# Attention and feed-forward on one core: the remainder of the exponential as the square of a logarithm, the sums over keys from one matrix product, the feed-forward's linear part as one matrix

## The chip, the cores and the metric

The program runs on one core of one Trainium2 chip, in one launch. The metric is the device time of one execution in microseconds. Three runs of the kernel before took 1280.52, 1281.53 and 1281.73 us; the median is 1281.53 us.

## The reference, cut to what matters

Keys and values are one tensor: `kv` is averaged over 4 x 4 places, which leaves 768 keys in each of the 4 batches, and multiplied by `w_sr`. Each batch has 12288 queries of 128 channels. A feed-forward layer with 2048 hidden units follows.

```
kv_pool = kv.reshape(B, H//4, 4, W//4, 4, C).mean(axis=(2, 4))
k = v = kv_pool.reshape(B, -1, C) @ w_sr              # 768 x 128 in each batch
s = (q @ k.T) / sqrt(C);  a = softmax(s)
x = a @ v                                             # 49152 tokens x 128
h = x @ w_in                                          # 2048 hidden units
return (h - tanh(h)) @ w_out
```

## The kernel before, in words

**The arithmetic.** Scores are small here, and so is the distance of a token's `x` from the mean of the values. The kernel subtracts the mean of the keys, and writes exp(s) as 1 + s + r. The part 1 contributes nothing to the centred values, the part s contributes a product of the query with one 128 x 128 matrix of the batch (`Mh`, the second moment of the values), and only the remainder r = exp(s) - 1 - s needs the work per key. In the same way h - tanh(h) is taken about the mean value: a constant and a slope (`At`, `Ah`, one matrix for the batch) and a rest, which is u * u * (u + 1) of a scaled u and needs the work per hidden unit. At the end a flag says whether the two approximations hold for these inputs (`NEAR`, `SPREAD`); if it is 0, a general path (`any_inputs`) computes everything again.

**The tiling.** A tile is 512 queries, channels on partitions; there are 24 tiles in a batch and 96 in all. A "wide" array has 128 x 1024 elements: 3 of them cover the 768 keys, 8 the 2048 hidden units. `big` is a ring of 3 wide PSUM buffers (2 banks each), `x` and `acc` are one bank each: that is all of PSUM.

**Attention of one tile** (`attention`). ScalarE rounds the query to fp32r (L879, `qr`), GpSimd forms what rounding left (L932, `ql`). For each of 3 wide arrays TensorE makes scores (L894, 2 matmuls), ScalarE the exponential (L898), VectorE the remainder r in fp16 (L901). The sum of the remainders over keys is needed for the softmax's denominator: from tile 2 on, the first array is copied by a DMA on SP's queue into `rs` and the other two are added to it by accumulating DMAs that GpSimd issues (L917); TensorE then sums `rs` over partitions with a matrix of ones (L922, 2 matmuls). ScalarE makes the factor 1/denominator from it (L942), the numerator is 6 matmuls with the fp16 values (L938) and 3 for the linear part in two precisions (L928), VectorE multiplies (L949), GpSimd rounds the result (L952) and forms the rest (L978).

**Feed-forward of one tile** (`feed_forward`). 16 matmuls make the hidden units, two to a `big` buffer (L1009). For 7 of the 8 wide arrays ScalarE squares (L1013) and VectorE multiplies (L1016). For the eighth (`ON_POOL`) ScalarE copies (L1020) and GpSimd does three operations (L1023, L1027 twice). 16 matmuls bring the result back (L1047), 3 add the linear part in two precisions (L998), ScalarE adds the constant (L1058), SP stores.

**Once per batch** (`keys`, `about_centre`): the pooled keys (DMAs that add on arrival, issued by GpSimd, L463), key and value matrices, moments, slopes and scaled weights. For batches 1 to 3 this work stands between the tiles of the batch before; for batch 0 it stands at the start.

**What sets the order.** All operations are first listed with a step (a place in time, 8 steps to a tile, table `AT`), an engine and a cost. `Plan.run` then plays them through once at build time and writes each engine's instructions in the order in which they started there. On the chip that order is fixed: an engine that waits holds up everything behind it on its queue. `lane` operations of an engine start in the order of their steps. `MOVES` shifts single operations of the start and of the batch work. Steps rank the work and are no times.

## Time and profile before

| | |
|---|---|
| span of the profiled execution | 1278.4 us |
| median of the three runs | 1281.53 us |
| TensorE busy | 1246.3 us (97%), 5424 matmuls |
| VectorE busy | 1220.1 us (95%), 1180 instructions |
| ScalarE busy | 1200.0 us (94%), 1426 |
| GpSimd busy | 1160.8 us (91%), 981 |
| granted TensorE clock, mean of the span | 0.995 |

The profile gives one time for the profiled execution, its span from the first to the last instruction; the median of the timed runs is 3.1 us above it. A busy share is the union of the instructions' spans. A matmul's listed duration (about 0.39 us) overlaps that of the next, so its cost is read as the distance from one start to the next; the same holds for short overlaps on the other engines. Of two spans on GpSimd that overlap, only the starts are exact.

### The profile page before, as it was taken

How to read it: one execution, taken by the hardware profiler on the slowest of the kernel's cores; microseconds unless marked ns; L12 is line 12 of the kernel's file. 1: busy time of each engine (PE TensorE's matmuls, PEld its weight loads, DVE VectorE, ACT ScalarE, POOL GpSimd, SP SyncE). 2: the span in 40 equal slices, each digit the busy share in tenths (PEclk: the TensorE clock that was granted, in tenths of full speed). 3: DMA queues.
4: the chain of work that ended last, by engine and by line, in shares of the span. 5: the costliest groups of instructions: out<-in, count | busy, mean ns of one | idle time of the engine just before them, and what ended most of it. 6: DMA issues, size and time to landing. Idle time of an engine off the chain costs nothing.

```text
span 1278.4 us, 17185 instructions
## 1 busy us (share of the span) xinstructions
PE 1246.3 (97%) x5424; PEld 869.0 (68%) x5424; DVE 1220.1 (95%) x1180; ACT 1200.0 (94%) x1426; POOL 1160.8 (91%) x981
## 2 busy tenths in 40 slices
PE   4999999999999999999999999999999999999997
PEld 3766766676667676676676666677767667676765
DVE  6899999999999999999999999999999999999996
ACT  4799999999999999999999999999999999999995
POOL 3689999999999998999999998999998888988886
PEclk9999999999999999999999999999999999999999
DMA  9376664555466673445556675344453434344431
GB/s 363 81 149 136 148 137 108 127 125 113 119 135 145 134 154 104 108 110 133 117 136 143 143 155 118 91 108 117 107 131 95 122 92 114 95 113 105 107 87 34
DMA packets 82706, 158.44 MB, mean 124 GB/s; under 512 B 9936, under 2 KB 12112, under 8 KB 82608
## 3 DMA queue, kind: packets, MB, share of 16 engines
q0 software_dynamic: 33552, 66.99, 30.9%
q1 hardware_dynamic: 49056, 90.29, 20.2%
q8 instruction: 44, 0.72, 0.2%
q14 instruction: 54, 0.44, 0.1%
HBM read 57.93 MB, written 25.39 MB: 65 GB/s over the span
## 4 chain that ended last, share of the span: by engine, by line
PE 86%; POOL 6%; DVE 4%; ACT 1%; issue 1%; DMA 1%; SPq 0%; POOLq 0%; DVEq 0%; ACTq 0%
PE big L1009 27%; PE acc L1047 25%; PE big L894 10%; PE x L938 9%; PE x L928 5%; PE acc L998 5%; PE x L922 3%; DVE r L1016 2%; POOL rp L1027 1%; POOL z L1027 1%; POOL kc L649 1%; PE x L806 1%; DMA rp<-in_kv_by_key_dram 1%; DVE r L901 1%; ACT u L1013 1%
## 5 line engine op out<-in xcount | busy, mean ns | idle before, releaser
L1016 DVE SCALAR_TENSOR_TENSOR r<-big,u 128x1024 fp32r<-128x1024 f32 x672 | 787.1, 1218 | 14.2 <-ACT u L1013 13.8
L1013 ACT ACTIVATE u<-big 128x1024 f32<-128x1024 f32 x672 | 671.6, 1029 | 27.6 <-PE big L1009 16.4
L1009 PE MATMUL big<-dr,winr 128*128 128x512 f32 x1536 | 519.4, 419 | 2.4 <-DVE r L901 1.3
L1047 PE MATMUL acc<-r,Wr 128*128 128x512 f32 x1344 | 412.3, 398 | 0.6 <-DVE r L1016 0.6
L901 DVE SCALAR_TENSOR_TENSOR r<-E,big 128x1024 f16<-128x1024 f32 x288 | 350.3, 1217 | 19.3 <-ACT E L898 18.7
L1009 PEld LDWEIGHTS big<-dr,winr 128*128 128x128 f32 x1536 | 272.0, 188 | 123.2 <-DVE r L1016 35.5
L898 ACT ACTIVATE E<-big 128x1024 f32<-128x1024 f32 x288 | 297.7, 1034 | 2.5 <-PE big L894 2.3
L1047 PEld LDWEIGHTS acc<-r,Wr 128*128 128x128 f32 x1344 | 251.1, 188 | 59.7 <-DVE r L1016 1.5
L1027 POOL TENSOR_TENSOR rp<-z,v 128x1024 fp32r<-128x1024 f32 x96 | 266.5, 2776 | 0.2
L1027 POOL TENSOR_TENSOR z<-z,v 128x1024 f32<-128x1024 f32 x96 | 239.1, 2490 | 0.1
L917 POOL DMA_DIRECT2D rs<-r x188 | 207.9, 1106 | 4.3 <-DMA left<-t 1.4
L894 PE MATMUL big<-qr,kTr 128*128 128x512 f32 x576 | 192.3, 416 | 3.1 <-DVE r L1016 3.0
L932 POOL TENSOR_TENSOR ql<-q,qr 128x512 fp32r<-128x512 f32 x96 | 187.2, 1950 | 5.6 <-ACT qr L879 5.6
L938 PE MATMUL x<-r,vvr 128*128 128x512 f16 x576 | 174.4, 384 | 0.0
L1023 POOL TENSOR_SCALAR z<-v 128x1024 f32<-128x1024 f32 x96 | 109.6, 1142 | 66.1 <-ACT v L1020 65.4
L978 POOL TENSOR_TENSOR dl<-df,dr 128x512 fp32r<-128x512 f32 x96 | 158.6, 1653 | 0.0
L894 PEld LDWEIGHTS big<-qr,kTr 128*128 128x128 f32 x576 | 100.7, 188 | 43.8 <-DVE r L1016 26.6
L1020 ACT COPY v<-big 128x1024 f32<-128x1024 f32 x96 | 97.5, 1016 | 8.2 <-PE big L1009 1.6
L938 PEld LDWEIGHTS <-vvr 128*128 128x128 f16 x576 | 33.4, 98 | 78.6 <-issue 78.5
L1047 PE MATMUL acc<-rp,Wr 128*128 128x512 f32 x192 | 77.6, 485 | 0.7 <-POOL rp L1027 0.7
L1058 ACT ACTIVATE o<-acc,At 128x512 f32<-128x512 f32 x96 | 65.5, 682 | 4.1 <-PE acc L1047 4.1
L952 POOL TENSOR_SCALAR dr<-df 128x512 fp32r<-128x512 f32 x96 | 68.5, 713 | 0.9 <-DVE df L949 0.7
(187 smaller groups left out, 1028.1 us busy)
## 6 DMA issues: line engine op xcount, KB each, us to landing
rs<-r POOLq DMA_DIRECT2D x188, 256.0 KB, 3.6
q<-in_q_dram SPq DMA_DIRECT2D x96, 256.0 KB
out_dram<-o SPq DMA_DIRECT2D x96, 256.0 KB
rs<-r SPq DMA_DIRECT2D x94, 256.0 KB
kvp<-in_kv_by_place_dram POOLq DMA_DIRECT2D x45, 384.0 KB, 5.9
r<-in_kv_by_key_dram SPq DMA_DIRECT2D x6, 512.0 KB
kc<-inverse SPq DMA_DIRECT2D x12, 256.0 KB
u<-in_moe_w_in_dram SPq DMA_DIRECT2D x3, 512.0 KB
```

The source lines that it names most:

```text
L894: PE.matmul(out=half(plan[s], h), lhsT=plan[kTr][:, n * P : (n + 1) * P], rhs=plan[qr], start=True, stop=True)
L898: A.activation(out=plan[e], in_=plan[s], func=AF.Exp)
L901: V.scalar_tensor_tensor(out=plan[r], in0=plan[e], scalar=-1.0, in1=plan[s], op0=ALU.add, op1=ALU.subtract)
L917: PL.dma_start(out=plan[rs], in_=plan[r2s[k]], accum_op=ALU.add)
L932: PL.tensor_tensor(out=plan[ql], in0=plan[qs], in1=plan[qr].bitcast(F32), op=ALU.subtract)
L938: PE.matmul(out=plan[num], lhsT=plan[vvr][:, n], rhs=half(plan[f"r2.{g}.{k}"], h), start=(start and h == 0), stop=(stop and h == 1))
L978: PL.tensor_tensor(out=plan[dl], in0=plan[df], in1=plan[dr].bitcast(F32), op=ALU.subtract)
L1009: PE.matmul(out=half(plan[hp], h), lhsT=plan[winr][:, f * P : (f + 1) * P], rhs=plan[dr], start=True, stop=True)
L1013: A.activation(out=plan[u], in_=plan[hp], func=AF.Square)
L1016: V.scalar_tensor_tensor(out=plan[r], in0=plan[hp], scalar=1.0, in1=plan[u], op0=ALU.add, op1=ALU.mult)
L1027: PL.tensor_tensor(out=plan[to], in0=plan[x], in1=plan[y], op=ALU.mult)
L1047: PE.matmul(out=plan[acc], lhsT=plan[Wr][:, 2 * n + h], rhs=half(plan[r], h), start=(start and h == 0), stop=(stop and h == 1))
```

## The change

It does seven things to each tile, and retimes the plan.

- The remainder is no longer exp(s) - 1 - s. ScalarE takes p = ln(1 - s/3), and p * p, times 4.5, agrees with it to the third order in s. The factor 4.5 and 1/768 go into the value matrix. The square is made by GpSimd (by VectorE in tiles 0 and 1), and is fp32r instead of fp16, as is the value matrix.
- The denominator no longer sums the remainders. TensorE makes y = `Mh` * q (one matmul), VectorE multiplies y with q (`along`), TensorE sums over channels (one matmul, `shares`). The transfers into `rs`, the SP copy and the two adding DMAs of each tile, are gone.
- The numerator keeps its 6 matmuls over keys; the 3 of the linear part are gone. ScalarE copies y, scaled, into `yk` (`linear`), VectorE makes the correction `dy` (`fewer`) and adds it to the numerator (`apart`), GpSimd adds `yk` and rounds (`rounded`).
- In the feed-forward the linear part is split: the product of the two linear maps (`Lh`, one matrix for the batch, in two precisions, 3 matmuls) acts on the query, and the slopes alone (`Ah`) act on the small rest `dl` (1 matmul). `Mh` and `Ah` have one precision now.
- All 8 wide arrays of the hidden layer are squared on ScalarE and multiplied on VectorE; the path through GpSimd is gone.
- GpSimd instead of ScalarE rounds the query; VectorE instead of ScalarE adds the constant to the result.
- Tiles 0 and 1 are outside the lanes, tiles 0 to 2 have places of their own in `MOVES`. All of `AT` and `MOVES` is new, buffer counts change, and the two thresholds of the flag are tighter.

```
-NEAR = 2.0**-12
-SPREAD = 0.09
+NEAR = 2.0**-12.5
+SPREAD = 0.06
...
-    DIRECT, HELD = 2, 6
-    BUFS = {"kc": 2, "kvp": 1, "kTr": 2, "vvr": 2, "Mn": 1, "Mh": 2, "A": 2, "Ah": 2, "Wg": 3, "Wr": 2,
-            "winr": 2, "q": 4, "qr": 5, "ql": 2, "E": 2, "r2": 7, "rs": 3, "t": 2, "dl": 1, "df": 1, "dr": 2, "u": 3, "r": 4,
...
+    HELD = 6
+    BUFS = {"kc": 2, "kvp": 1, "kTr": 2, "vvr": 2, "Mn": 2, "Mh": 2, "A": 2, "Ah": 2, "Lh": 2, "L32": 1, "Wg": 3, "Wr": 2,
+            "winr": 2, "q": 4, "qr": 5, "ql": 4, "p": 2, "r2": 5, "m": 1, "yk": 3, "t": 2, "dy": 2, "dl": 2, "dr": 2, "u": 3, "r": 4,
...
-        sb(vvr, "vvr", [P, KT, C], F16)
+        sb(vvr, "vvr", [P, KT, C], R32)
         sb(Mn, "Mn", [P, C])
         Mh = f"Mh.{b}"
-        sb(Mh, "Mh", [P, 2, C], R32)
+        sb(Mh, "Mh", [P, C], R32)
...
-                V.tensor_scalar(out=to, in0=plan[pv][:, 0:K], scalar1=1.0 / W, scalar2=None,
+                V.tensor_scalar(out=to, in0=plan[pv][:, 0:K], scalar1=4.5 / (W * K), scalar2=None,
                                 op0=ALU.mult)
             else:
-                A.activation(out=to, in_=plan[pv][:, 0:K], func=AF.Copy, scale=1.0 / W)
+                A.activation(out=to, in_=plan[pv][:, 0:K], func=AF.Copy, scale=4.5 / (W * K))
...
-            A.copy(out=plan[Mh][:, 0], in_=plan[Mn])
-
-        def moment_left():
-            PL.tensor_tensor(out=plan[Mh][:, 1], in0=plan[Mn], in1=plan[Mh][:, 0].bitcast(F32),
-                             op=ALU.subtract)
+            A.copy(out=plan[Mh], in_=plan[Mn])
...
+            A.copy(out=plan[Ah], in_=plan[Am])
+        def joined_slopes():
+            PE.matmul(out=plan[pl][:, 0:P], lhsT=plan[Mn], rhs=plan[Am], start=True, stop=True)
+
+        def upper_joined():
+            A.activation(out=plan[L32], in_=plan[pl][:, 0:P], func=AF.Copy, scale=1.0 / K)
+            A.copy(out=plan[Lh][:, 0], in_=plan[L32])
+
+        def lower_joined():
+            PL.tensor_tensor(out=plan[Lh][:, 1], in0=plan[L32], in1=plan[Lh][:, 0].bitcast(F32),
                              op=ALU.subtract)
...
+        plan.op(both, "PE", 0.25, joined_slopes, (Mn, Am), (pl,), late=0.2)
+        plan.op(both, "ACT", 0.65, upper_joined, (pl,), (L32, Lh), late=0.1)
+        plan.op(both, "POOL", 0.35, lower_joined, (L32, Lh), (Lh,))
...
-        forth=[5.006, 6.77, 1.949, -0.24, 6.099, 6.377, -0.744, 0.701],
-        first=[5.679, 9.22, 4.356, 3.056, 5.989, 8.157, 2.847, 3.419],
-        then=[-0.595, 13.719, 9.033, 8.413, 13.098, 13.284, 7.905, 8.745],
-        back=[11.194, 8.84, 7.059, 6.464, 7.496, 8.395, 6.207, 7.041],
-        scores=[-23.029, -18.269, -20.751], exps=[-19.961, -18.018, -18.625],
-        beyond=[-15.248, -11.082, -12.106], values=[-6.756, -5.007, -2.334], more=[1.5, 2.327],
-        num=-7.419, copied=31.229, added=[-22.279, -20.144], shares=-7.436, left=-4.833,
-        straight=-4.347, apart=4.414, rounded=-7.164, rounded_q=-22.319, slope=5.811,
+        forth=[2.45, 3.464, 3.695, 1.438, 5.156, 6.569, 6.117, 0.003], first=[1.573, 2.307, 4.773,
+        1.131, 4.896, 7.31, 5.944, -0.169], then=[3.15, 3.826, 5.428, 2.061, 6.694, 7.185, 6.772,
+        0.143], back=[6.79, 7.363, 8.439, 5.797, 8.925, 9.908, 9.425, 3.441], scores=[-14.749,
+        -11.301, -13.599], roots=[-15.296, -11.109, -14.823], beyond=[-13.898, -8.14, -13.687],
+        values=[-3.116, -3.646, -3.759], num=-3.84, y=-16.182, linear=-15.661, along=-15.804,
+        shares=-13.446, left=-14.305, fewer=-13.812, straight=2.577, apart=-2.145, rounded=-0.77,
+        rounded_q=-19.108, slope=4.928, result=8.935, lower_q=-14.73, acc=3.001)
...
+    ALONE, OWN_PLACE = 2, 3
+
+    def put(name, g, s0, n=None):
+        step = s0 + (AT[name] if n is None else AT[name][n])
+        return step if g >= OWN_PLACE else at(step, *(("g", name, g) if n is None else ("g", name, n, g)))
...
-            A.copy(out=plan[qr], in_=plan[qs])
-        behind = ("held",) if g < ago + 3 else (f"first.{g - ago}",)
+            PL.tensor_scalar(out=plan[qr], in0=plan[qs], scalar1=1.0, scalar2=1.0, op0=ALU.mult,
+                             op1=ALU.mult)
+
+        behind = ("held",) if g < 6 else (f"left.{g - 6}",)
+        plan.op(put("rounded_q", g, s0) - 7, "SP", 0.5, load_q, behind, (qs,), late=1.0, dma=0.71)
...
-            def exps(s=s, e=e):
-                A.activation(out=plan[e], in_=plan[s], func=AF.Exp)
-
-            def beyond(s=s, e=e, r=r):
-                V.scalar_tensor_tensor(out=plan[r], in0=plan[e], scalar=-1.0, in1=plan[s],
-                                       op0=ALU.add, op1=ALU.subtract)
...
-        def copied():
-            SP.dma_start(out=plan[rs], in_=plan[r2s[0]])
-
-        def added(k):
-            PL.dma_start(out=plan[rs], in_=plan[r2s[k]], accum_op=ALU.add)
...
+            def roots(s=s, p=p):
+                A.activation(out=plan[p], in_=plan[s], func=AF.Ln, scale=-1.0 / 3, bias=ones[:, 0:1])
+
+            def beyond(p=p, r=r):
+                (PL if g >= ALONE else V).tensor_tensor(out=plan[r], in0=plan[p], in1=plan[p], op=ALU.mult)
+
+            plan.op(put("scores", g, s0, k), "PE", 0.463, scores, (kTr, qr), (s,), late=0.196, lane=g >= ALONE)
+            plan.op(put("roots", g, s0, k), "ACT", 0.926, roots, (s,), (p,), late=0.14, lane=g >= ALONE)
+            plan.op(put("beyond", g, s0, k), *(("POOL", 2.4) if g >= ALONE else ("DVE", 1.14)), beyond, (p,), (r,),
+                    port=True, lane=g >= ALONE)
...
+        def upper_linear():
+            PE.matmul(out=plan[y], lhsT=plan[Mh], rhs=plan[qr], start=True, stop=True)
+
+        def linear():
+            A.activation(out=plan[yk], in_=plan[y], func=AF.Copy, scale=1.0 / K)
+
+        def along():
+            V.tensor_tensor(out=plan[m], in0=plan[y], in1=plan[qs], op=ALU.mult)
...
-            of = [rs] if g >= DIRECT else r2s
-            for n in range(2 * len(of)):
-                PE.matmul(out=plan[den], lhsT=share, rhs=half(plan[of[n // 2]], n % 2),
-                          start=(n == 0), stop=(n == 2 * len(of) - 1))
-
-        def straight(start, stop):
-            upper, lower = (plan[Mh][:, n] for n in range(2))
-            for n, (x, y) in enumerate(((upper, qr), (lower, qr), (upper, ql))):
-                PE.matmul(out=plan[num], lhsT=x, rhs=plan[y], start=(start and n == 0),
-                          stop=(stop and n == 2))
+            PE.matmul(out=plan[den], lhsT=share, rhs=plan[m], start=True, stop=True)
+
+        def share_left():
+            A.activation(out=plan[t], in_=plan[den], func=AF.Copy, scale=-0.5 * scale / K)
+
+        def store_left():
+            SP.dma_start(out=left[g : g + 1], in_=plan[t][0:1, :])
+
+        def fewer():
+            V.scalar_tensor_tensor(out=plan[dy], in0=plan[den], scalar=-0.5 * scale / K, in1=plan[yk],
+                                   op0=ALU.mult, op1=ALU.mult)
 
         def lower_q():
             PL.tensor_tensor(out=plan[ql], in0=plan[qs], in1=plan[qr].bitcast(F32),

...
-            V.tensor_tensor(out=plan[df], in0=plan[num], in1=plan[t], op=ALU.mult)
+            V.tensor_tensor(out=plan[dl], in0=plan[num], in1=plan[dy], op=ALU.add)
 
         def rounded():
-            PL.tensor_scalar(out=plan[dr], in0=plan[df], scalar1=1.0, scalar2=1.0, op0=ALU.mult,
-                             op1=ALU.mult)
+            PL.tensor_tensor(out=plan[dr], in0=plan[dl].bitcast(F32), in1=plan[yk], op=ALU.add)
...
-            upper, lower = (plan[Ah][:, n] for n in range(2))
-            for n, (x, y) in enumerate(((upper, dr), (lower, dr), (upper, dl))):
+            upper, lower = (plan[Lh][:, n] for n in range(2))
+            for n, (x, y) in enumerate(((upper, qr), (lower, qr), (upper, ql))):
                 PE.matmul(out=plan[acc], lhsT=x, rhs=plan[y], start=(start and n == 0),
                           stop=(stop and n == 2))
 
-        terms = [(AT["slope"], 0.7, straight, (Ah, dl, dr))]
+        def slope(start, stop):
+            PE.matmul(out=plan[acc], lhsT=plan[Ah], rhs=plan[dl], start=start, stop=stop)
+
+        terms = [(put("straight", g, s0), 0.695, straight, (Lh, qr, ql)), (put("slope", g, s0), 0.232, slope, (Ah, dl))]
...
-            if n in ON_POOL:
-                sb(r, "rp", [P, WIDE], R32, step=then)
-                sb(v, "v", [P, WIDE], step=first)
-                sb(z, "z", [P, WIDE], step=then)
-                plan.op(first, "ACT", 0.905, copy, (hp,), (v,), late=0.14, lane=True)
-                plan.op(then, "POOL", 1.1, moved_pool, (v,), (z,), lane=True)
-                for to, at in zip((z, r), AT["more"]):
-                    plan.op(s0 + at, "POOL", 2.41, partial(times, to, z, v), (z, v), (to,), lane=True)
...
-            A.activation(out=plan[o], in_=plan[acc], func=AF.Identity, bias=plan[At][:, C : C + 1])
+            V.tensor_scalar(out=plan[o], in0=plan[acc], scalar1=plan[At][:, C : C + 1], scalar2=None,
+                            op0=ALU.add)
...
-    PRO = (2, 0, 0)
-    AGO = 3
+    PRO = (0, 0, 0)
```

## Rows read from the trace of the kernel before

**Rows 1.** Windows of the trace: stretch, its us, busy time (instructions) of PE, PEld, DVE, ACT, POOL; clock, DMA share, GB/s.
```profile
0.00:60.00 60.00, 41.16 (x239) 32.97 (x240) 47.85 (x87) 34.70 (x55) 27.77 (x38) 0.94 0.68 229
...
353.00:656.00 303.00, 301.63 (x1302) 209.42 (x1300) 294.21 (x277) 292.72 (x348) 290.95 (x247) 1.00 0.56 129
...
959.00:1262.00 303.00, 302.68 (x1298) 210.70 (x1297) 292.90 (x271) 291.34 (x338) 264.07 (x209) 1.00 0.40 99
```

**Rows 2.** The page: the chain that ended last, by engine.
```profile
PE 86%; POOL 6%; DVE 4%; ACT 1%; issue 1%; DMA 1%; SPq 0%; POOLq 0%; DVEq 0%; ACTq 0%
```

**Rows 3.** Timeline of TensorE: start, us to the last end, engine, line, operation, count.
```profile
1140.02 0.60 PE L922 MATMUL x<-rs,share 128*128 128x512 f16 x2
...
1147.50 0.63 PE L1047 MATMUL acc<-r,Wr 128*128 128x512 f32 x2
1147.96 0.63 PE L1009 MATMUL big<-dr,winr 128*128 128x512 f32 x2
...
1152.31 0.60 PE L922 MATMUL x<-rs,share 128*128 128x512 f16 x2
1152.56 0.81 PE L1009 MATMUL big<-dr,winr 128*128 128x512 f32 x2
1153.22 0.62 PE L1047 MATMUL acc<-r,Wr 128*128 128x512 f32 x2
```

**Rows 4.** Timeline of VectorE in the same tile.
```profile
1145.64 1.22 DVE L901 SCALAR_TENSOR_TENSOR r<-E,big 128x1024 f16<-128x1024 f32 x1
1146.78 0.68 DVE L949 TENSOR_TENSOR df<-x,t 128x512 f32<-128x512 f32 x1
1147.66 1.22 DVE L901 SCALAR_TENSOR_TENSOR r<-E,big 128x1024 f16<-128x1024 f32 x1 [0.20 <-ACT E L898]
```

**Rows 5.** Timeline of ScalarE in the same tile, and its first instruction.
```profile
0.81 1.28 ACT L359 ACT_TABLE_LOAD   x1 [0.81 <-PEq L1308]
...
1144.02 0.68 ACT L1058 ACTIVATE o<-acc,At 128x512 f32<-128x512 f32 x1
1144.59 1.02 ACT L898 ACTIVATE E<-big 128x1024 f32<-128x1024 f32 x1
...
1152.96 0.60 ACT L942 ACTIVATE t<-x 128x512 f32<-128x512 f32 x1
1153.45 1.04 ACT L1013 ACTIVATE u<-big 128x1024 f32<-128x1024 f32 x1
1154.35 1.05 ACT L898 ACTIVATE E<-big 128x1024 f32<-128x1024 f32 x1
```

**Rows 6.** Timeline of GpSimd in the same tile.
```profile
1146.87 1.04 POOL L1023 TENSOR_SCALAR z<-v 128x1024 f32<-128x1024 f32 x1 [1.61 <-ACT v L1020]
1147.89 0.61 POOL L952 TENSOR_SCALAR dr<-df 128x512 fp32r<-128x512 f32 x1
1148.47 2.41 POOL L1027 TENSOR_TENSOR z<-z,v 128x1024 f32<-128x1024 f32 x1
1150.83 0.88 POOL L917 DMA_DIRECT2D rs<-r  x1
1151.47 2.69 POOL L1027 TENSOR_TENSOR rp<-z,v 128x1024 fp32r<-128x1024 f32 x1
1153.84 1.55 POOL L978 TENSOR_TENSOR dl<-df,dr 128x512 fp32r<-128x512 f32 x1
1155.06 1.16 POOL L917 DMA_DIRECT2D rs<-r  x1
```

**Rows 7.** Groups by line: count, busy us, mean ns of one, idle before it by releaser.
```profile
L1009 PEld LDWEIGHTS big<-dr,winr 128*128 128x128 f32 x1536 | 272.0, 188 | 123.2 <-DVE r L1016 35.5 <-DVE r L901 27.8 <-PE acc L1047 1.0
...
L1027 POOL TENSOR_TENSOR rp<-z,v 128x1024 fp32r<-128x1024 f32 x96 | 266.5, 2776 | 0.2
...
L938 PEld LDWEIGHTS <-vvr 128*128 128x128 f16 x576 | 33.4, 98 | 78.6 <-issue 78.5
```

**Rows 8.** Windows, ScalarE's L1058 alone (one for each tile): stretch, busy (count), clock.
```profile
353.00:656.00 303.00, 16.37 (x24) 1.00 0.56 129
```

More of the change, by code (lines that the diff above doesn't have):

```diff
@@ L293, in attention_then_ffn @@
     ones = const.tile([P, P], F32, name="ones")
-    share = const.tile([P, P], F16, name="share")
+    share = const.tile([P, P], R32, name="share")
     ident = const.tile([P, P], F32, name="ident")
@@ L308, in fill @@
             V.memset(ones, 1.0)
-            V.memset(share, 1.0)
+            V.tensor_scalar(out=share, in0=ones, scalar1=1.0, scalar2=None, op0=ALU.mult)
         def cut():
@@ new lines, in attention @@
+        sb(m, "m", [P, G], R32, step=put("along", g, s0))
+        sb(dy, "dy", [P, G], step=put("fewer", g, s0))
+        bank(y, "x", put("y", g, s0))
+        bank(den, "x", put("shares", g, s0))
+        bank(num, "x", put("num", g, s0))
+        def upper_linear():
[4 more added lines that the diff above has]
+            V.tensor_tensor(out=plan[m], in0=plan[y], in1=plan[qs], op=ALU.mult)
@@ L951, in rounded @@
         def rounded():
-            PL.tensor_scalar(out=plan[dr], in0=plan[df], scalar1=1.0, scalar2=1.0, op0=ALU.mult,
-                             op1=ALU.mult)
+            PL.tensor_tensor(out=plan[dr], in0=plan[dl].bitcast(F32), in1=plan[yk], op=ALU.add)
         r2s = [f"r2.{g}.{k}" for k in range(AN)]
-        plan.tile(f"first.{g}", f"first.{g}", 1, lambda: None)
-        if g >= DIRECT:
-            plan.op(s0 + AT["copied"], "SP", 0.5, copied, (r2s[0],), (rs,), late=1.7, dma=0.69)
-            for k in range(1, AN):
-                to = (rs, f"first.{g}") if k == 1 else (rs,)
-                plan.op(s0 + AT["added"][k - 1], "POOL", 0.9, partial(added, k), (r2s[k],), to,
-                        late=0.81, dma=1.7, lane=True)
@@ L963, in attention @@
-        plan.op(s0 + AT["shares"], "PE", 0.455 if g >= DIRECT else 1.36, shares,
-                ["ident"] + ([rs] if g >= DIRECT else r2s), (den,), late=0.196, lane=True)
-        plan.op(s0 + AT["left"], "ACT", 0.49, share_left, (den,), (t,), late=0.14, lane=True)
-        plan.op(s0 + AT["left"] + 1, "SP", 0.5, store_left, (t,), (f"left.{g}",), late=2.0, dma=0.02)
-        plan.op(s0 + AT["lower_q"], "POOL", 1.25, lower_q, (qs, qr), (ql,), lane=True)
-        terms = [(AT["values"][k], 0.465, partial(values, k), (vvr, r2s[k])) for k in range(AN)]
@@ L969, in attention @@
-        terms.append((AT["straight"], 0.695, straight, (Mh, qr, ql)))
+        plan.op(put("y", g, s0), "PE", 0.232, upper_linear, (Mh, qr), (y,), late=0.196, lane=g >= ALONE)
+        plan.op(put("linear", g, s0), "ACT", 0.49, linear, (y,), (yk,), late=0.14, lane=g >= ALONE)
+        plan.op(put("along", g, s0), "DVE", 0.62, along, (y, qs), (m,), late=0.2, lane=g >= ALONE)
+        plan.op(put("shares", g, s0), "PE", 0.232, shares, ("ident", m), (den,), late=0.196, lane=g >= ALONE)
+        plan.op(put("left", g, s0), "ACT", 0.49, share_left, (den,), (t,), late=0.14, lane=g >= ALONE)
@@ L970, in attention @@
+        plan.op(put("left", g, s0) + 1, "SP", 0.5, store_left, (t,), (f"left.{g}",), late=2.0, dma=0.02)
+        plan.op(put("lower_q", g, s0), "POOL", 1.25, lower_q, (qs, qr), (ql,), lane=g >= ALONE)
+        plan.op(put("fewer", g, s0), "DVE", 0.66, fewer, (yk, den), (dy,), late=0.2, lane=g >= ALONE)
+        terms = [(put("values", g, s0, k), 0.465, partial(values, k), (vvr, r2s[k])) for k in range(AN)]
         terms.sort(key=lambda x: x[0])
         for n, (at, us, emit, of) in enumerate(terms):
-            plan.op(s0 + at, "PE", us, partial(emit, start=(n == 0), stop=(n == AN)), of, (num,),
+            plan.op(at, "PE", us, partial(emit, start=(n == 0), stop=(n == AN - 1)), of, (num,),
@@ L973, in attention @@
                     late=0.196, lane=True)
-        plan.op(s0 + AT["apart"], "DVE", 0.72, apart, (num, t), (df,), late=0.2, lane=True)
-        plan.op(s0 + AT["rounded"], "POOL", 0.59, rounded, (df,), (dr,), lane=True)
-        def lower_left():
-            PL.tensor_tensor(out=plan[dl], in0=plan[df], in1=plan[dr].bitcast(F32), op=ALU.subtract)
-        plan.op(s0 + AT["lower_left"], "POOL", 1.25, lower_left, (df, dr), (dl,), lane=True)
+        plan.op(put("apart", g, s0), "DVE", 0.66, apart, (num, dy), (dl,), late=0.2, lane=g >= ALONE)
@@ L982, in attention_then_ffn @@
+        plan.op(put("rounded", g, s0), "POOL", 1.25, rounded, (dl, yk), (dr,), lane=g >= ALONE)
     EARLY = (4, 1.6, 7, 3, 5, 9, 18, 8)
```

114 lines of the change are left out of this document (44 added, 70 removed), and 130 rows, old and new, of the table MOVES.

## The prediction, made before the changed kernel was built or run

> **What bounds the kernel now.** I read the windows first. After a start of 60 us, in which TensorE is busy for only 41, every engine is above 85%: in 353 to 656 us TensorE has 301.6 of 303, VectorE 294, ScalarE 293, GpSimd 291; in the last 24 tiles only GpSimd falls, to 264 [rows 1]. The chain that ended last puts 86% on TensorE [rows 2]. So a tile's period is the thing to explain, and the timelines of one tile without batch work give it: TensorE reaches the same instruction at 1140.02 and 1152.31, a period of 12.29 us [rows 3]. There are 95 such steps and some batch work: 24 tiles with it take 303 us, 8 more than 24 periods [rows 1, 8].
>
> What fills the 12.29? Pairs of fp32r matmuls start 0.46 to 0.47 apart, so 0.2325 each; two fp16 and two fp32r take 0.91, so fp16 costs about 0.2225 [rows 3]. A tile has 44 of the first kind and 8 of the second: 10.23 + 1.78 = 12.01. TensorE stands still for 0.28 in each tile. VectorE's wide operation takes 1.14 from start to start, its 512-wide one 0.68 less the 0.08 that neighbours overlap, 0.60: ten and one make 12.00, and the listed wait of 0.20 is on ScalarE [rows 4]. So two engines are level at 12.0, and the 0.28 is what their waiting for each other costs: the weight loads of L1009 waited 35.5 and 27.8 us for VectorE to release `big` [rows 7].
>
> **The change, engine by engine, per tile from tile 2 on.**
>
> TensorE loses 3 + 3 + 2 matmuls (linear part of the numerator, of the feed-forward, old sum) and gains y, the new sum, 3 with `Lh` and 1 with `Ah`: 52 becomes 50, and all are fp32r: 50 x 0.2325 = 11.63, against 12.01. The values' weights load in 188 ns as fp32r instead of 98 as fp16 [rows 7]; that is below the 232 between matmuls and lies beside them, as it does for L1009. If it showed, 6 x 0.09 would cost 0.54 a tile; I take 0, since L1009 and L1047 load such weights at this pace [rows 3].
>
> VectorE loses three remainders and the old multiply, and gains the eighth hidden array, `along`, `fewer`, the new `apart` and `result`: 8 x 1.14 + 4 x 0.60 = 11.52, against 12.00. Each of the four reads PSUM, as L949 does, and L949 is the row for them; I bound each between 0.55 and 0.68 (11.3 to 11.8).
>
> ScalarE keeps 11 wide operations. A square takes 0.90 (1153.45 to 1154.35). The logarithm isn't in the trace: by the exponential, 0.90 to 1.05, and with an operand for its bias, which makes L1058 0.57 where L942 has 0.49, I take 1.00. The rounded query and the result go, `linear` comes: 8 x 0.90 + 3 x 1.00 + 2 x 0.49 = 11.2 [rows 5]. Dearer logarithms matter from 0.2 each; ScalarE has 0.7 to spare.
>
> Logarithm, square and copy must then be at hand without a reload. The trace has one table load, 1.28 us, in the whole program, though exponential, square, copy and identity alternate [rows 5]. The Trainium skill ("ScalarE: Activation LUTs", Table sets) says that functions lie in named sets, that a switch to another set is a load, and names ln's set with exp, and copy and identity as in every set; the square it doesn't name there. By that rule, if square were missing beside ln, each tile would pay six loads; the trace can't tell. That is rival E.
>
> GpSimd loses the moved cube (1.02 + 2.36 + 2.37), two DMA issues (0.62 to 0.64) and L952 (0.58), and gains the rounding of the query (0.58, as L952) and three squares. Nearest rows for a square: L1027, the same operation on two arrays, 2.36 from start to start (1148.47 to 1150.83, 1151.47 to 1153.84) [rows 6], with a mean span of 2.78 [rows 7]; a one-input pass takes 1.02. So between 1.02 and 2.78; I take 2.36, the same form. `rounded` becomes a two-input 512-wide operation like L978 (1.22), `lower_q` stays at 1.22: 0.58 + 1.22 + 3 x 2.36 + 1.22 = 10.1, against 1.02 + 0.58 + 4.73 + 1.26 + 2 x 1.22 = 10.03 [rows 6]. Its load is unchanged while the others' falls by 0.4.
>
> DMA: three transfers a tile go. None was late (the adding DMAs' receiver, L922, follows without a gap) [rows 3], so I book nothing for the path, and nothing for the SP queue. `q` loads now wait for the flag's row of six tiles before, long past.
>
> **What waits newly.** Scores now wait for GpSimd to round the query, and the first hidden matmuls for `rounded`, both queued behind squares of 2.36 us in a fixed order. By the steps, `rounded` stood 6.4 before the first `forth` and stands 0.8 before it now: a GpSimd that lags stops TensorE at once. In the other direction three of eleven `big` buffers are free after ScalarE instead of after VectorE, which takes a VectorE operation of 1.14 out of three of eleven holds. `x` is written three times a tile instead of twice, each read by VectorE; two single matmuls with two readers hold it for about 0.39 + 0.60 + 0.49 each, six with one reader for 1.4 + 0.2 + 0.6: 5 us of 12, so no bound.
>
> **The sum.** The floor falls from 12.01 to 11.63. I keep 0.24 of the 0.28 lost in waiting, since the floors fall alike: 11.87 a tile, 0.42 x 95 = 39.9 us less. Batch work: GpSimd had 291 busy of 303; 24 x 0.07 more makes 293, and the batch's tiles should now take 303 - 24 x 0.42 = 293. That is full by this row; but the row counts overlapped spans. In the last batch 264 were busy where starts give 24 x 10.03 = 241, so some 23 too many: 270 by starts [rows 1, 6]. I book 2 us a batch, 6, between 0 and 12. The joined matrix is one small matmul, two small copies and one small subtraction a batch, beside ScalarE's slack: 0, at most 1 a batch. Start and end: by the steps a tile stretches from -19 to 9 instead of -23 to 13, a tile less of filling and draining, but most of the start is loads and weights; I take -4, between -12 and +4. 1278.4 - 39.9 + 6 - 4 = 1240.5 of span. The median of the runs lies 3.1 above the profiled span; so **1244**.
>
> **The rivals.**
>
> B, all waits go: with a freer `big` the period comes to 11.70, 56 us less, no batch charge: 1278.4 - 56 - 4 + 3.1 = 1222. For it: three early releases, VectorE at 11.52. Against: before, level floors cost 0.28.
>
> C, GpSimd sets the batches: it may not go above the 96% it has in a batch (291 of 303). Then 293 / 0.96 = 305 for each batch with work, +2 against before; only the last batch gains, 10: 1278.4 + 6 - 10 - 4 + 3.1 = 1274. For it: the short lead of `rounded`. Against: the 23 us of overlap in the row.
>
> D, slower: the squares cost their span, 2.78, because GpSimd can't overlap them; 3 x 0.42 x 24 = 30 a batch. Its load becomes 300 by starts or 323 by spans; at 312, three batches are 9 longer each: 1278.4 + 27 - 10 - 4 + 3.1 = 1295. It turns to slower where the middle of both counts (282) reaches 303: 0.30 more a square, 2.66 us. Against it: 2.36 twice in one tile [rows 6].
>
> E, the logarithm doesn't share a table: six loads of 1.28 make ScalarE's tile 11.2 + 7.7 = 18.9; 96 x 7.0 = 675 more, about 1920. Also here, that the change doesn't do what it says because the tighter flag sends it to the general path. From the reference's inputs the mean square remainder is at most 1.33e-4 (limit 1.73e-4), and the second condition reaches 0.79 of its limit in batch 0: it holds.
>
> **How the numbers follow.** Forecast (1230 to 1256) 0.60, B 0.15, C 0.13, D 0.10, E 0.02. A measurement tells 0.2%, 2.6 us, from no change. Faster: 0.60 + 0.15 + 0.06 of C (which with its bounds reaches past 1279) = 0.81; same 0.07 of C; slower 0.12. The range goes from a little below B to C: 1218 to 1276 leaves out D, E, the upper part of C (0.05) and the lowest of B (0.03): 0.10 + 0.02 + 0.05 + 0.03 = 0.20.
>
> **What would show it.** Right: a period of 11.8 to 11.95 at TensorE late in the program, GpSimd's squares 2.36 apart, one table load. GpSimd without idle time and TensorE waiting for `dr` or `qr` between 60 and 960 us would be C; squares over 2.66 apart, D; a period of 11.7 or less, B. The forecast is wrong if the period stays above 12.1, or if the batch work's 8 us a batch doubles.

## The result, and the profile after

The changed kernel takes 1288.67 us (median of 4 runs, 1286.68 to 1290.74), the kernel before 1281.36 in the same comparison: ratio 1.0059, 95% interval 1.0045 to 1.0074. It is 0.6% slower, where I had forecast 1244 us and had given slower a chance of 0.12.

The profiled run took 1286.68 us, its span is 1285.0, 6.6 more than before. The windows, in the columns of [rows 1]:

```profile
353.00:656.00 303.00, 301.59 (x1260) 223.21 (x1259) 288.61 (x301) 288.81 (x326) 246.80 (x197) 1.00 0.27 66
959.00:1262.00 303.00, 300.57 (x1237) 220.81 (x1235) 287.39 (x295) 287.08 (x318) 210.60 (x155) 1.00 0.13 40
```

A batch's 303 us hold 24 tiles, as before. VectorE and ScalarE have 4 to 6 us less to do, GpSimd 44 less, DMA moves half as much; TensorE's row still says 301.6 [rows 1]. The lighter load is there and bought nothing. TensorE's share of the chain that ended last falls from 86% [rows 2] to 79%; other engines and standing have come into it. Below stand this chain and then the timelines of TensorE, VectorE, ScalarE and GpSimd over one tile of the last batch (start, us, engine, line, operation, count, idle time before and who ended it):

```profile
PE 79%; DVE 5%; issue 4%; ACT 3%; POOL 3%; DMA 0%; SPq 0%; DVEq 0%; ACTq 0%
```
```profile
1148.41 1.20 PE L998 MATMUL x<-r,vvr 128*128 128x512 f32 x4
1149.45 0.62 PE L948 MATMUL big<-qr,kTr 128*128 128x512 f32 x2
1149.91 0.62 PE L998 MATMUL x<-r,vvr 128*128 128x512 f32 x2
1150.37 0.39 PE L1044 MATMUL acc<-dl,Ah 128*128 128x512 f32 x1
1150.60 0.73 PE L1054 MATMUL big<-dr,winr 128*128 128x512 f32 x2
...
1160.70 1.19 PE L998 MATMUL x<-r,vvr 128*128 128x512 f32 x4
```
```profile
1147.04 0.68 DVE L988 SCALAR_TENSOR_TENSOR dy<-x,yk 128x512 f32<-128x512 f32 x1
...
1149.31 2.36 DVE L1061 SCALAR_TENSOR_TENSOR r<-big,u 128x1024 fp32r<-128x1024 f32 x2 [0.33 <-ACT u L1058]
...
1152.42 4.62 DVE L1061 SCALAR_TENSOR_TENSOR r<-big,u 128x1024 fp32r<-128x1024 f32 x4 [0.15 <-ACT u L1058]
1156.95 0.68 DVE L976 TENSOR_TENSOR m<-x,q 128x512 fp32r<-128x512 f32 x1
1157.55 0.74 DVE L1084 TENSOR_SCALAR o<-acc,At 128x512 f32<-128x512 f32 x1
1158.21 1.21 DVE L1061 SCALAR_TENSOR_TENSOR r<-big,u 128x1024 fp32r<-128x1024 f32 x1
1159.34 0.68 DVE L988 SCALAR_TENSOR_TENSOR dy<-x,yk 128x512 f32<-128x512 f32 x1
```
```profile
0.81 1.28 ACT L403 ACT_TABLE_LOAD   x1 [0.81 <-PEq L1333]
...
43.79 1.28 ACT L952 ACT_TABLE_LOAD   x1
...
1146.71 1.02 ACT L1058 ACTIVATE u<-big 128x1024 f32<-128x1024 f32 x1
1147.75 0.60 ACT L982 ACTIVATE t<-x 128x512 f32<-128x512 f32 x1
1148.25 1.94 ACT L1058 ACTIVATE u<-big 128x1024 f32<-128x1024 f32 x2
...
1151.36 2.87 ACT L1058 ACTIVATE u<-big 128x1024 f32<-128x1024 f32 x3
...
1157.99 1.12 ACT L952 ACTIVATE p<-big,ones 128x1024 f32<-128x1024 f32 x1
1159.00 1.01 ACT L1058 ACTIVATE u<-big 128x1024 f32<-128x1024 f32 x1
1160.06 0.60 ACT L982 ACTIVATE t<-x 128x512 f32<-128x512 f32 x1
```
```profile
1152.35 1.29 POOL L1005 TENSOR_TENSOR dr<-dl,yk 128x512 fp32r<-128x512 f32 x1 [2.97 <-DVE dl L1002]
1153.61 1.89 POOL L955 TENSOR_TENSOR r<-p 128x1024 fp32r<-128x1024 f32 x1
1155.46 1.32 POOL L992 TENSOR_TENSOR ql<-q,qr 128x512 fp32r<-128x512 f32 x1
```

TensorE's values (L998) come at 1148.41 and 1160.70: the period is 12.29, as before [rows 3]. Its work is what I had counted: pairs 0.46 apart, so 50 matmuls take 11.63, and it stands for 0.66 a tile where it stood for 0.28. The busy columns hide that: a matmul is shown with 0.39 to 0.40 where the next can start after 0.23, so a pause of 0.15 leaves no gap in them. Distances from start to start show it (L998's four take 1.04 here, 0.93 without a stall).

What holds the period can be read off these rows as a loop, a chain of waits that leads from an instruction back to itself in the next tile. `dy` starts at 1147.04; `t`, which reads the same PSUM tile `den`, at 1147.75, 0.03 after `dy` has ended (1147.04 + 0.68), though the square ahead of it started at 1146.71 and such squares give way after 0.92, at 1147.63; `t` releases the bank, and L998 starts 0.66 later; from there TensorE has its matmuls in a row up to the hidden pair at 1150.60 (2.19); its square starts 0.76 later, the cube of that 1.06 later, at 1152.42; then VectorE has five cubes, `m` and `o` in a row, 6.92, to the next `dy` at 1159.34. Together 0.71 + 0.66 + 2.19 + 0.76 + 1.06 + 6.92 = 12.30. No engine is full, but once a tile this chain closes. A second branch is as long: from `t` to ScalarE's square at 1148.25 (0.50), its cube at 1149.31 (1.06), and the hidden pair that takes the buffer which this cube frees (1.29), 2.85 like 0.66 + 2.19. Both branches start at `t`. The wait of `t` itself is only 0.12 long; that bounds what its removal can give before ScalarE's own row holds `t`.

That `t` and `dy`, two readers, wait for one another is in neither the reference nor the plan (which counts a wait only where one of two uses writes). The Trainium skill says why such a wait is in the program ("PSUM — Partial Sum Buffer", PSUM bank collisions raise a hardware error): two engines may not touch a bank's partitions at once, reads included, and since nothing in the chip holds one of them back, the program has to put them in order. No run here shows such a collision. In the change `t` starts 0.03 to 0.05 after the end of `dy` in 91 of 96 tiles, and in each run in which both read `den` they never overlap.

The list of waits (engine, operation, line, releaser: us, times, longest) has the reader's wait where TensorE feels it, before the values' weights:
```profile
POOL dr L1005 <- DVE dl L1002: 206.2, 88, 8.7
DVE r L1061 <- ACT u L1058: 49.8, 188, 1.6
...
PEld x L998 <- ACT t L982: 37.4, 90, 0.6
```

Where the 6.6 come from, by the starts of `o`: the first is at 79.80, before at 78.21; the three batches with work take 305.8, 305.2 and 305.2, before 305.7, 305.4 and 305.1; the last 282.7, before 277.5. So only the last batch lost, and in it the last tiles, here on VectorE in the changed kernel and on ScalarE in the kernel before:
```profile
1231.30 0.74 DVE L1084 TENSOR_SCALAR o<-acc,At 128x512 f32<-128x512 f32 x1
...
1267.98 0.75 DVE L1084 TENSOR_SCALAR o<-acc,At 128x512 f32<-128x512 f32 x1
1278.67 0.75 DVE L1084 TENSOR_SCALAR o<-acc,At 128x512 f32<-128x512 f32 x1 [0.82 <-PE acc L1073]
```
```profile
1230.02 0.69 ACT L1058 ACTIVATE o<-acc,At 128x512 f32<-128x512 f32 x1
...
1263.09 0.68 ACT L1058 ACTIVATE o<-acc,At 128x512 f32<-128x512 f32 x1
1271.88 0.69 ACT L1058 ACTIVATE o<-acc,At 128x512 f32<-128x512 f32 x1 [3.70 <-PE acc L1047]
```
The last four steps take 41.9 from 1230.02 in the kernel before and 47.4 from 1231.30 now. Before, the attention ran further ahead: its last scores start 39.8 before the last `o`, now 30.7, so that more of the last tiles have no attention beside them.

### The profile page after: what moved, and what is told of

The parts are those of the page before. It is cut to its first block, busy times and chain, and to the rows that moved or that the text cites. A ratio compares the mean times of both kernels' runs of the same rounds, so it can differ in the third digit from the quotient of the medians.

```text
span 1285.0 us, 16882 instructions
## 1 busy us (share of the span) xinstructions
PE 1246.5 (97%) x5232; PEld 924.9 (72%) x5232; DVE 1199.7 (93%) x1282; ACT 1179.6 (92%) x1339; POOL 972.7 (76%) x782
## 4 chain that ended last, share of the span: by engine, by line
PE 79%; DVE 5%; issue 4%; ACT 3%; POOL 3%; DMA 0%; SPq 0%; DVEq 0%; ACTq 0%
PE big L1054 25%; PE acc L1073 23%; PE x L998 11%; PE big L948 10%; PE acc L1040 5%; DVE r L1061 3%; ACT u L1058 2%; PE acc L1044 2%; PE x L970 2%; PE x L979 1%; POOL kc L690 1%; PE x L847 1%; DVE o L1084 1%; POOL dr L1005 0%; ACT p L952 0%
## 5 line engine op out<-in xcount | busy, mean ns | idle before, releaser
L1061 DVE SCALAR_TENSOR_TENSOR r<-big,u 128x1024 fp32r<-128x1024 f32 x768 | 906.3, 1218 | 59.1 <-ACT u L1058 49.8
L1058 ACT ACTIVATE u<-big 128x1024 f32<-128x1024 f32 x768 | 755.9, 1024 | 55.4 <-PE big L1054 48.8
L955 POOL TENSOR_TENSOR r<-p 128x1024 fp32r<-128x1024 f32 x282 | 536.1, 1909 | 46.3 <-ACT p L952 38.1
L952 ACT ACTIVATE p<-big,ones 128x1024 f32<-128x1024 f32 x288 | 321.7, 1117 | 4.7 <-PE big L948 3.4
L1005 POOL TENSOR_TENSOR dr<-dl,yk 128x512 fp32r<-128x512 f32 x96 | 125.0, 1302 | 208.7 <-DVE dl L1002 206.2
L998 PE MATMUL x<-r,vvr 128*128 128x512 f32 x576 | 174.8, 412 | 3.3 <-DVE r L955 1.7
L998 PEld LDWEIGHTS x<-r,vvr 128*128 128x128 f32 x576 | 100.9, 188 | 58.3 <-ACT t L982 37.4
L1084 DVE TENSOR_SCALAR o<-acc,At 128x512 f32<-128x512 f32 x96 | 71.2, 742 | 0.9 <-PE acc L1073 0.8
L988 DVE SCALAR_TENSOR_TENSOR dy<-x,yk 128x512 f32<-128x512 f32 x96 | 65.3, 680 | 3.6 <-PE x L979 2.5
L1002 DVE TENSOR_TENSOR dl<-x,dy 128x512 fp32r<-128x512 f32 x96 | 65.4, 681 | 0.8 <-PE x L998 0.8
```

The lines of the kernel that those rows point to most:

```text
L952: A.activation(out=plan[p], in_=plan[s], func=AF.Ln, scale=-1.0 / 3, bias=ones[:, 0:1])
L955: (PL if g >= ALONE else V).tensor_tensor(out=plan[r], in0=plan[p], in1=plan[p], op=ALU.mult)
L998: PE.matmul(out=plan[num], lhsT=plan[vvr][:, n], rhs=half(plan[f"r2.{g}.{k}"], h), start=(start and h == 0), stop=(stop and h == 1))
L1005: PL.tensor_tensor(out=plan[dr], in0=plan[dl].bitcast(F32), in1=plan[yk], op=ALU.add)
L1058: A.activation(out=plan[u], in_=plan[hp], func=AF.Square)
L1061: V.scalar_tensor_tensor(out=plan[r], in0=plan[hp], scalar=1.0, in1=plan[u], op0=ALU.add, op1=ALU.mult)
```

## The experiments

Period: the usual distance between starts of `o` among tiles 80 to 92. All ratios are to the kernel before.

| run | us | ratio [95%] | period |
|---|---|---|---|
| the change | 1288.7 | 1.0059 [1.0045, 1.0074] | 12.29 |
| e1_lead | 1299.8 | 1.0149 [1.0132, 1.0166] | 12.29 |
| e5_reader | 1277.4 | 0.9983 [0.9970, 0.9995] | 12.18 |
| e4_copy | 1285.5 | 1.0040 [1.0027, 1.0052] | 12.30 |
| e2_pooldy | 1317.5 | 1.0285 [1.0268, 1.0302] | 12.1 |
| e6_reader_lead | 1284.6 | 1.0032 [1.0022, 1.0042] | 12.12 |
| e9_reader_copy | 1264.2 | 0.9869 [0.9853, 0.9886] | 12.03 |
| e7_order | 1293.3 | 1.0100 [1.0083, 1.0117] | 12.02 |
| e10_less_pe | 1286.5 | 1.0042 [1.0028, 1.0057] | 12.29 |
| e8_order | 1265.9 | 0.9884 [0.9868, 0.9901] | 12.08 |
| e8_best | 1333.8 | 1.0404 [1.0384, 1.0425] | 12.66 |
| e12_operand | 1359.3 | 1.0610 [1.0593, 1.0628] | 12.83 |

The theories: *reader*, the loop above; *lead*, that the short way from `dl` over `dr` to the hidden matmuls holds TensorE up, as my rival C had feared; *level*, that three engines at 95% cost half a microsecond in any order.

**e1_lead.** The attention part of each tile one tile earlier:
```diff
+        step = s0 + (AT[name] ...) - (EARLIER if name in AHEAD_OF else 0)   # EARLIER = 8
```


> All fifteen attention steps of a tile stand 8 steps (one tile) earlier, so that `rounded` has about 8.8 steps of lead before the first `forth` instead of 0.8; the order of the steps within a period is as it was. The lead theory (TensorE waits for dl, dr and the first matmuls after them, because the change shortened this way): the period falls from 12.29 to 11.9 or less and the time to 1245 to 1255, even with a tile more of filling (some 10 us in it). The reader theory (the copy `t` of ScalarE stands until VectorE's `fewer` has read the same PSUM tile, which closes a loop of one tile's length): the period stays at 12.2 to 12.3, and the time is 1287 to 1300. The level theory (three engines at 11.4 to 11.7 cost 0.6 of waiting whatever their order): the same as the reader theory.

The period stayed. It is no clean test of the lead, though. The edit also moved one instruction of the start, tile 2's rounding of the query (its place in `MOVES` from -117 to -17), and the first `o` comes at 97.8, 18 later than in the change; so the time says little, and the period is what to read. And from its list of waits (engine, line, releaser: us, times, longest), `dr` now waits for its buffer, which the last tile's hidden matmuls hold:
```profile
POOL dr L1008 <- PE big L1057: 222.6, 86, 8.5
```

**e5_reader.** One wait less, every instruction at its old place:
```diff
-                A.activation(out=plan[t], in_=plan[den], ...)
+                A.activation(out=plan[t], in_=plan[yk], ...)
```


> ScalarE's copy `t` reads `yk` from SBUF instead of the PSUM tile `den`, at its old place in the order; this leaves the sums over keys, and so the flag's test, wrong, and nothing else. The work of each engine and its order stay; only the order between two readers of `den` goes. The reader theory: `t` no longer stands until VectorE's `fewer` is done, the period falls from 12.29 to about 12.05 and the time by 0.24 x 95, to 1260 to 1268. The lead theory: TensorE waits for dr as before, 12.25 to 12.29, 1284 to 1289. The level theory: the waits move elsewhere, 12.2 to 12.3, 1280 to 1289.

0.11 of the period went instead of 0.24, and 0.76% of the time: a little more than level allows (12.18 against 12.2, 1277 us against 1280), and less than I said. It is about what the wait of `t` was long. The wait of TensorE for `t` is gone from the list; a second loop stands behind it. Its trace, VectorE and ScalarE:
```profile
1147.34 0.68 DVE L1002 TENSOR_TENSOR dl<-x,dy 128x512 fp32r<-128x512 f32 x1
...
1157.24 2.36 DVE L1061 SCALAR_TENSOR_TENSOR r<-big,u 128x1024 fp32r<-128x1024 f32 x2 [0.21 <-ACT u L1058]
1159.51 0.68 DVE L1002 TENSOR_TENSOR dl<-x,dy 128x512 fp32r<-128x512 f32 x1
```
```profile
1150.28 1.03 ACT L1058 ACTIVATE u<-big 128x1024 f32<-128x1024 f32 x1 [0.28 <-PE big L1054]
1151.20 0.59 ACT L973 ACTIVATE yk<-x 128x512 f32<-128x512 f32 x1
1151.74 1.12 ACT L952 ACTIVATE p<-big,ones 128x1024 f32<-128x1024 f32 x1
1152.76 1.01 ACT L1058 ACTIVATE u<-big 128x1024 f32<-128x1024 f32 x1
1153.74 1.12 ACT L952 ACTIVATE p<-big,ones 128x1024 f32<-128x1024 f32 x1
...
1156.18 1.94 ACT L1058 ACTIVATE u<-big 128x1024 f32<-128x1024 f32 x2
```
`dl` at 1147.34 gives `dr`, the hidden pair and the square that starts at 1150.28 (2.94); ScalarE goes without a pause, with two logarithms among its operations, to the square at 1156.18 (5.90); the cube that waits for that one starts 1.06 later, and after two cubes (2.27) comes the next `dl`: 12.17.

**e4_copy.** ScalarE's three logarithms as plain copies (no logarithm is computed):
```diff
-    A.activation(out=plan[p], in_=plan[s], func=AF.Ln, scale=-1.0 / 3, bias=ones[:, 0:1])
+    A.activation(out=plan[p], in_=plan[s], func=AF.Copy, scale=-1.0 / 3)
```


> The logarithm with its bias operand becomes a plain scaled copy; this leaves out the logarithm, so the remainders are wrong. ScalarE's three eviction passes should then take about 0.90 start to start instead of 1.01: 0.33 a tile less on ScalarE, everything else as it was. The level theory: a third of a microsecond off one of three level engines shows, 0.1 to 0.3 of the period, time 1260 to 1279. The reader and the lead theories: the loop doesn't hold a logarithm (the reader's one holds six cubes, two squares and the copy; the lead's one holds the values and two small sums), so the period stays within 0.05 and the time at 1283 to 1289.

Nothing on the period. ScalarE, earlier now, shows the reader's wait openly:
```profile
ACT t L982 <- DVE dy L988: 18.3, 71, 1.0
```

**e9_reader_copy.** The edits of e5_reader and e4_copy together.

> Again two edits together that were run apart: `t` copies `yk` (sums over keys wrong) and the logarithm is a plain copy (remainders wrong). Apart, the first took 11 us off the change's time and the second 3. The loop theory: the logarithms lie in the second loop, which shows only when the reader's wait is gone; so 0.1 off each of two or three logarithms now counts, the period falls from 12.17 to 12.0 to 12.08, and the time to 1262 to 1270, more than the sum of the two edits. The level theory: the two gains add up, 14 to 15 us under the change, 1273 to 1276, period 12.12 to 12.17.

The sharpest test. Apart, the two took 0.76% and 0.19% off the change's ratio; together 1.90%, twice the sum. Loads would add up; loops don't: a logarithm costs nothing while the first loop is longer, and most of its price when it isn't (0.15 of the period, for two that lie in the second loop and became some 0.1 shorter each). The reader theory had both numbers in its ranges, the level theory neither.

**e10_less_pe.** TensorE's part:
```diff
-   enumerate(((upper, qr), (lower, qr), (upper, ql)))
+   enumerate(((upper, qr), (upper, ql)))
...
-   stop=(stop and n == 2))
+   stop=(stop and n == 1))
```


> One of the three matmuls of the linear term, that of the query's rounding error, is left out (so the linear term is less exact): TensorE has 49 instead of 50 matmuls a tile, 0.23 us less to do, nothing else changes. The prediction's way of counting (the busiest engine's load plus what its waiting cost) and the level theory: some or all of 0.23 comes off the period of 12.29, so 12.06 to 12.2 and 1266 to 1280. The loop theory: that matmul doesn't lie in the loop (dy, t, values, first scores and hidden matmuls, square, five cubes, dy); TensorE only stands longer, the period stays at 12.27 to 12.30, the time at 1285 to 1290.

The edit leaves out another matmul than the expectation names: `lower` times `qr`, the part with what rounding left of the matrix `Lh`; that with the query's rounding error (`ql`) stays. The load taken away is the same, and the order of the others too. TensorE's busy time in the last 303 us fell from 300.6 to 295.3, and the period stayed to the hundredth:
```profile
959.00:1262.00 303.00, 295.34 (x1214) 216.65 (x1213) 287.70 (x295) 287.78 (x318) 211.95 (x156) 1.00 0.12 41
```

**e6_reader_lead.** e5 and e1 together.

> Both edits of before in one: `t` copies `yk` instead of `den` (the sums over keys, and so the flag's test, are wrong), and the attention steps stand a tile earlier. With the reader's wait gone the period was 12.17, and the trace of that run shows a second loop: VectorE's last cube, dl, dr, TensorE's first matmuls from dr, and then ScalarE's row of squares, logarithms and copies to the square that this cube waits for. The loop theory: the early dr cuts this loop at its middle, and the period falls to 12.0 to 12.1; the time is not below 1277, since a tile more has to be filled (that edit alone cost some 14 us). The level theory (three engines at 11.5 to 11.7 cost half a microsecond whatever the order): 12.17 to 12.3.

12.12, just beyond the range: 0.06 better than the reader's edit alone, 0.17 better than the lead alone. `dr` waits for its buffer as in e1_lead, so how much a free lead would give is still open.

**e2_pooldy.** A way to drop the second reader and leave nothing out:
```diff
-  V.scalar_tensor_tensor(out=plan[dy], in0=plan[den], scalar=..., in1=plan[yk], ...)
+  PL.tensor_tensor(out=plan[dy], in0=plan[t], in1=plan[yk], op=ALU.mult)
```


> The multiply `fewer` goes to GpSimd and takes the copy `t` in place of `den`, so that `den` has one reader; VectorE loses 0.60 a tile, GpSimd gains a two-input pass of about 1.25 and has the slack for it (206 us waiting for dl alone). The reader theory: the period falls to about 12.05 (1260 to 1270), less what GpSimd's longer queue costs in the batches, which the plan overstates (it counts a square 2.4, the trace 1.86): up to 25 us dearer, so 1260 to 1290, with the last batch's period as the clean sign. The level theory: VectorE falls to 10.9 of busy time, the period to 11.8 to 12.0. The lead theory: dr is no earlier, the period stays at 12.2 to 12.3.

The clean sign came (12.1 in the last batch), and VectorE's 0.6 less brought no 11.9, against level. But the time rose beyond my range: in the batches with work single tiles took 20.3 and 21.8. There GpSimd has the batch's work, `dy` and squares in one queue, which I take for the cause without a test; VectorE's wait for ScalarE's squares, 49.8 us in the change, grew:
```profile
DVE r L1060 <- ACT u L1057: 116.5, 268, 4.1
```

**e7_order and e8_order.** The instructions of the change, laid in another order: new steps for the tile (e7), and for the batch work and first tiles as well (e8). The order was searched with the durations and waits of these traces, the readers' wait among them, and the plan's prices set to them:
```diff
-    ALONE, OWN_PLACE = 2, 3
+    ALONE, OWN_PLACE = 2, 0
+    NEXT = dict(left=-17.085, fewer=-16.231, apart=-5.86, rounded=-5.345, ...)      # e7
+        of = NEXT if g >= OWN_PLACE else AT
-   "ACT", 0.926, roots ... ("POOL", 2.4)
+   "ACT", 1.01, roots ... ("POOL", 1.87)
...
```


> The same instructions on the same engines as in the change, with the steps of the tile (and the plan's prices: 1.87 for GpSimd's square, 1.01 for the logarithm, small ones as traced) laid anew, by a search over orders in which a read of a PSUM tile waits for the other engine's read of it, and a buffer goes to whoever comes next. The loop theory: loads don't hold the period, the order of the steps does; the period without batch work falls to 11.9 to 11.95, which the sum of the prediction had; the last 20 tiles take 238 instead of 246. The level theory: 12.2 to 12.3 in any order. The time as a whole is open in both: the steps of the batch work were laid for the old order, and I expect 1272 to 1286.

> As in the run with a new order of the tile's steps, the same instructions on the same engines as in the change; now the steps of the batch work (keys, weights, slopes) and of the first tiles are laid anew too, by the same search, which takes durations and waits from the traces and lets a read of a PSUM tile wait for the other engine's read. The loop theory: the period without batch work stays at 12.0 as in that run, and a batch's 24 tiles take some 300 instead of 307; first result at 80 to 84, 1255 to 1264 in all. The level theory: what the batch work costs beside three engines at 95% can't be ordered away; 1285 to 1293 as in that run.

e7 has the shorter period (12.02; I had said 11.9 to 11.95) and lost it again: its first `o` comes at 88.4, its batches take 309, 308 and 307, and the time is beyond my 1272 to 1286. With the batch work laid for it too, e8 takes 1265.9 (two more than I gave it; its period is 12.08 instead of 12.0), 1.2% faster than the kernel before and 1.7% than the change, with the same work. In both orders `t` stands ahead of `dy`, which starts 0.7 after `t` has ended, so the reader's wait is out of the loop. Windows of e8:
```profile
353.00:656.00 303.00, 301.39 (x1283) 227.52 (x1282) 292.35 (x306) 291.15 (x332) 247.55 (x199) 1.00 0.27 67
959.00:1262.00 303.00, 295.92 (x1234) 220.54 (x1232) 291.27 (x299) 282.77 (x309) 204.42 (x157) 1.00 0.12 42
```
Its batches take 301.7, 299.7, 298.7 and 274.4. Of the kernels that leave nothing out it is the fastest.

**e8_best and e12_operand.** In `fewer`, `den` (PSUM) replaced by `t` (SBUF), still on VectorE; e8_best with an order searched for that, e12 in e8_order's order (the tiles' instructions stand as there, a few of the start and the batch work differ):
```diff
-  V.scalar_tensor_tensor(out=plan[dy], in0=plan[den], scalar=..., in1=plan[yk], ...)
+  V.tensor_tensor(out=plan[dy], in0=plan[t], in1=plan[yk], op=ALU.mult)
```


> The order laid anew as in the other run of this call, and one operand changed: `fewer` on VectorE multiplies `t` (SBUF) by `yk` instead of reading `den` again, so `den` has one reader and its bank is free after ScalarE's copy. Work per engine is the same. The loop theory: with this edge gone an order with a shorter loop exists: 11.9 a tile (the prediction's 11.87), a batch some 298, 1250 to 1262 in all, 2% under the kernel before. The level theory: 12.2 to 12.3 and 1277 or more. If ordering matters but the reader's edge doesn't, it equals the other run within 0.2%.

> The order that took 1266, and in it only the operand that the slow run had changed: `fewer` on VectorE multiplies `t` by `yk`, both in SBUF, where it read `den` from PSUM. The theory from that slow run's trace (VectorE's multiply of two SBUF operands and GpSimd's two-operand passes hold each other up; there the multiply took 949 ns on average instead of 681, and a square beside it 2.25 us instead of 1.90): both numbers show again, some 0.3 to 0.4 us a tile on GpSimd's path, and the time rises to 1275 to 1310. The rival (the slow run was slow by its own order of steps, and the operand is free): 1262 to 1268, the multiply at 0.68, since by the order alone nothing else changes.

Both are far slower: e8_best 72 us above the loop theory's range, e12 49 above the one that I gave it. The operand isn't free. The group of `dy` (count, busy us, mean ns, idle before it) in e8_order; then in e12_operand, with `m`, which is the same operation with one operand in PSUM, and the shortest, median and longest `dy`; and one tile of e12 on VectorE and GpSimd:
```profile
L976 DVE SCALAR_TENSOR_TENSOR dy<-x,yk 128x512 f32<-128x512 f32 x96 | 65.4, 681 | 3.5 <-PE x L967 3.5
```
```profile
L976 DVE TENSOR_TENSOR dy<-t,yk 128x512 f32<-128x512 f32 x96 | 176.8, 1842 | 2.9 <-ACT t L970 2.9
L964 DVE TENSOR_TENSOR m<-x,q 128x512 fp32r<-128x512 f32 x96 | 65.0, 677 | 1.5 <-ACT yk L961 1.4
...
L976 DVE TENSOR_TENSOR dy<-t,yk x96: 683/1698/8541, 51.0 to 1317.2; 128x512 f32<-128x512 f32 x96
```
```profile
1163.19 1.73 DVE L976 TENSOR_TENSOR dy<-t,yk 128x512 f32<-128x512 f32 x1
1164.84 1.21 DVE L1048 SCALAR_TENSOR_TENSOR r<-big,u 128x1024 fp32r<-128x1024 f32 x1
```
```profile
1163.05 1.32 POOL L979 TENSOR_TENSOR ql<-q,qr 128x512 fp32r<-128x512 f32 x1
1164.55 3.97 POOL L943 TENSOR_TENSOR r<-p 128x1024 fp32r<-128x1024 f32 x2 [0.18 <-ACT p L940]
```
GpSimd's `ql` runs until 1164.37; `dy`, begun 0.14 after it, ends at 1164.92, 0.55 after `ql` and thus about its own length later, and the next operation follows at once. It stood until GpSimd had finished, on average 1.16 us (1842 against 681 ns). Three times it took 7.3 to 8.5, while GpSimd ran five or six operations in a row. The square of 2.25 was another order's: in e8_best `dy` mostly began first, and 74 squares begun beside it took 2.25 on average, the others 1.92; here 68 such squares took 2.08, the others 1.94. Who begins second waits.

## Why the prediction was wrong, step by step

- **The step that failed** is "I keep 0.24 of the 0.28 lost in waiting, since the floors fall alike". The waiting came to 0.66, so the whole 0.38 that TensorE's floor lost came back as waiting and the term of -39.9 us was 0. Here the loads don't make the waiting; the longest loop does, and its length is worked out from the order of the instructions, not from anyone's load. e4_copy, e10_less_pe and e9_reader_copy show it, and e8_order, which has the same instructions in another order, a period of 12.08 and 23 us less. The change had put a new instruction (`fewer`) into the row of VectorE's operations, and a new edge (`t` after `fewer`) from there back to TensorE. That edge alone is worth 0.11 of the 0.42 that I had forecast. The lowest period of any run is 12.02 (e7_order), so that 0.15 above the forecast 11.87 stays open: no run shows what holds it.
- **The sentence beside it**: of `x` I wrote that two readers hold it in turn for 0.60 and 0.49, "5 us of 12, so no bound". The price was right, the reading wrong: a buffer that is free for most of the period can still close a loop, if its next writer is the next thing that everyone waits for. I asked how long it was held and not when it came free.
- The floors were right but for ScalarE's: pairs of fp32r matmuls 0.46 apart, weight loads of 188 ns beside them, VectorE's cubes 1.14 and its small ones 0.60 to 0.66 apart, the logarithm 1.01 (I took 1.00). Squares took 0.92 where I had 0.90, so ScalarE's floor is some 11.4 instead of 11.2, still under TensorE's. My sign of one table load was not met: there are two, the second at 43.79 ahead of the first logarithm, which the kernel before doesn't have. None comes after it, so logarithm, square and copy alternate without a reload; it takes 1.28 us once, and rival E is out.
- The square on GpSimd was mis-sized: 1.85 to 1.87 from start to start instead of 2.36, a tile's load 8.7 instead of 10.1. It decided nothing: GpSimd waited 206 us for `dl` alone. Rivals C and D, which had it as the bound, fall; that the time came out near D's 1295 is chance, since its cause isn't there.
- Batch work: +6 booked, 0 measured (three batches take 916.2 in both kernels). That it costs 8 us a batch was read too low: by the starts of `o` a batch takes 305.4, 24 periods 295, so 10, in both kernels. Start and end: -4 booked for a tile that stretches over fewer steps, +6.6 measured: the first `o` 1.6 later, the last batch 5.2 longer, what follows the last `o` 0.2 shorter. I saw a shorter stretch as less to fill and empty; but the tiles that run out without attention beside them are quick ones, 11.7 to 8.8, and the change has fewer of them. 1.6 + 5.2 - 0.2 is all of the span's 6.6.
- Rival B had the right lever (waiting, not load) and the wrong sign.

Whether the kernel before was held at its 12.29 by a loop of its own, as its 0.28 suggests, was not tried.

## What to carry to other kernels

Where engines are level and their orders fixed, follow one period of the profile backwards from an instruction to itself in the tile before: which edge lies in that loop decides what a lighter engine is worth, and it can be nothing. Count two engines' reads of one PSUM tile as an edge in the order in which they stand. To find out whether an engine bounds, take work from it and look whether the period moves; and test two suspected waits together as well as apart, since the second shows only when the first is gone.
